# Batch 0's softmax on [(h n), tokens] rows, with its sums and its spreads by matmul

## The chip, the cores and the metric

The kernel runs on one NeuronCore of a Trainium2 chip. The metric is the time of one execution on the device, in microseconds (us). The core has five engines that work side by side, each through its own instructions in order: PE (TensorE, matrix products into PSUM), DVE (VectorE), ACT (ScalarE), POOL (GpSimd) and SP (SyncE, which only issues transfers here). PEld in the profile is the loading of PE's weights, which overlaps PE.

## The reference

Per batch b and head h there are 512 tokens of 64 values (`x`) and 32 state rows of 64 values (`state`). Attention runs both ways between them, and what both read goes through a two-layer network with a leaky ReLU.

```python
B, H, S, Ns, D = (8, 8, 512, 32, 64)
scores = scale * np.matmul(x, state.transpose(0, 1, 3, 2))
scores = scores - scores.max(-1, keepdims=True)
a = np.exp(scores)
a /= a.sum(-1, keepdims=True) + 1e-09
xread = np.matmul(a, state)
scores2 = scale * np.matmul(state, x.transpose(0, 1, 3, 2))
...
sread = np.matmul(a2, x)
attn = np.concatenate([xread, sread], axis=2)
...
h = x @ w_in          # x: attn as rows of H*D = 512; w_in is 512 x 2048
g = np.maximum(0.01 * h, h)
return g @ w_out      # w_out is 2048 x 512
```

The change is in the first of the two softmaxes: for each token and head, over the 32 state rows, for batch 0 alone.

## The kernel before, in words

All of it is one hand-written order: the order in the text is the order on each engine, and a tile framework adds the semaphores and the rotation of buffers. PSUM has four names with buffers (`tag`): `sc` (one buffer of two banks), `big` (one of two banks), `ph` and `py` (two of one bank each). A new tile of a tag waits until the old one in its buffer has been read.

The first layer never forms `xread`. Per batch and group of four heads g, the 128 rows (head, state row), written (h n), hold the probabilities `aT` [128 rows, 512 tokens], and `M` = state times `w_in` [128 rows, 2048] is made by `a_m(a, c, tag)` in four blocks c of 512 columns (eight 64*32 matmuls each) and copied to SBUF in bf16 by `m_evict(a, c, pm, copy)`, where `copy` names the engine (`VEC`, `SCA`). The first layer is then, per 128 columns of w_in, two matmuls of `M` and `aT` that add in PSUM, and a leaky ReLU on ACT. The second layer is cut into `piece`s: tile i of 128 tokens, quarter jq of the 16 blocks, four matmuls each.

From batch 1 on, scores stand in PSUM as [(h n), tokens] (`a_scores`), and VectorE finds the maximum and the sum over 32 rows with 32x32 transposes (`a_shift`, `a_probs`: L216, L224, L226, L238, L242, L245, L247, L248; `a_max2`, L266 and L268, is of the second softmax).

Batch 0's start is on its own lines. Its x comes in two halves (`x0_half`, `xt0_evict`). `scores0(u)` puts the scores of head group u with tokens on partitions (`sct`, [128 tokens, 16 pairs of token tile and head, 32 state rows]). VectorE then takes the maximum over the last axis (`max0`, L454) and subtracts it (`sub0`, L459), ACT takes the exponential (`exp0`, L463), VectorE sums (L467), adds 1e-9 (L468), takes the reciprocal (L471) and multiplies (L473, all in `probs0`). The result has tokens on partitions, so PE transposes it (`at0_t`, L477) and a copy on ACT or DVE brings it to `a0.aT` (L520, L546). `spin(n, tag)` issues n matmuls of zeros (L126) in places where PE would stand still. Between these stand the transposes of all states (`state_t`, L155, and `state_evict`, L164), which the scores and M of batches 1 to 7 need, and blocks of M of batches 0 and 1.

The first layer of batch 0 starts with g=0 for the first pair of columns as soon as half of `aT` is there, and with g=1 when the other half is (`ff1_0`, L533). Then come pairs j = 2, 4, ... 14, whose PSUM is `big` for j = 2, 6, 10 (one ACT instruction for both, L554) and two `ph` banks otherwise (two, L540). Between the pairs stand blocks of M (batch 0: c = 2 after j=2, c = 3 after j=6; batch 1: c = 2 after j=10, c = 3 after j=12; all copied by VectorE) and batch 0's second scores. After the loop come the casts of batch 1's x (`cast_x`, L99, half on DVE, half on POOL), its transposes (L188, copies L579), its scores, its softmax on DVE, and 56 matmuls of `piece` around them; then batch 1's first layer (`ff1`, L347) starts. Batch 2's x is cast on POOL (L99) when it has come.

Loads of the weights and of x for batches 1 and 2 are issued by POOL (L112, L118, L93), in this order: four of w_in with two casts between, one of w_out, x of batch 1, three of w_out, x of batch 2.

Of the kernel before, what the change touches and what calls it, by code (L numbers as in the profile page):

```python
# [9 lines left out]
P = 128  # L10
B, H, S, D = 8, 8, 512, 64
NS = 32
# [3 lines left out]
NT = S // P  # L16
NK = H // 2
SCALE = 1.0 / (D ** 0.5)

BF16 = mybir.dt.bfloat16  # L20
FP32 = mybir.dt.float32
AF = mybir.ActivationFunctionType
ALU = mybir.AluOpType
AX = mybir.AxisListType
# [3 lines left out]
def kernel(  # L28
# [9 lines left out]
    nc = tc.nc  # L38

    consts = ctx.enter_context(tc.tile_pool(name="consts", bufs=1))  # L40
    wpool = ctx.enter_context(tc.tile_pool(name="wpool", bufs=1))
    xpool = ctx.enter_context(tc.tile_pool(name="xpool", bufs=4))
    att = ctx.enter_context(tc.tile_pool(name="att", bufs=2))
# [3 lines left out]
    psum = ctx.enter_context(tc.tile_pool(name="psum", bufs=2, space=bass.MemoryType.PSUM))  # L47
# [5 lines left out]
    VEC, SCA, POO = nc.vector.tensor_copy, nc.scalar.copy, nc.gpsimd.tensor_copy  # L53
# [22 lines left out]
    ident = consts.tile([P, P], BF16, name="ident")  # L76
# [3 lines left out]
    for u in range(2):  # L80
        for g in range(2):
# [2 lines left out]
                ident[:].rearrange("p (k v q) -> p k v q", k=NK, v=2)[:, 2 * u:2 * u + 2, g],  # L84
            )

    w_in_bf = wpool.tile([P, NK, DFF], BF16, name="w_in_bf")
    w_out_bf = wpool.tile([P, 16, DM], BF16, name="w_out_bf")
    xs, xl = {}, {}

    def load_x(b, eng):
        xl[b] = xpool.tile([P, H, NT * D], FP32, name="xl", tag="xl", bufs=2)
        eng.dma_start(xl[b][:], x[b].rearrange("h (p t) d -> p h (t d)", t=NT))  # L93

    def open_xb(b):
        xs[b] = xpool.tile([P, NT, H, D], BF16, name="xb", tag="xb")
# [24 lines left out]
        )  # L121

    def spin(n, tag):
        p = psum.tile([P, S], FP32, name="pspin", tag=tag)
        for _ in range(n):
            nc.tensor.matmul(p[:], lhsT=idle[:, :P], rhs=idle[:], start=True, stop=True)  # L126

# [2 lines left out]
    stbd = consts.tile([P, NK, 2, NS], BF16, name="stbd")  # L130
# [43 lines left out]
    def a_open(a, b):  # L174
        a.b = b
        a.xb = xs[b]
        a.xT = att.tile([P, NT, NK, P], BF16, name="xT", tag="xT")
# [79 lines left out]
    def a_exp(a):  # L257
        a.e1 = block_exp(a.sh, NB)

    def a_probs(a):  # L260
        a.aT = att.tile([P, 2, S], BF16, name="aT", tag="aT")
        block_probs(a.aT[:], a.e1, NB)
# [51 lines left out]
    def a_m(a, c, tag):  # L314
        if c == 0:
            a.M = mpool.tile([P, 2, DFF], BF16, name="M", tag="M")
        if tag == "py":
            pm = [psum.tile([P, DM], FP32, name="pm", tag="py") for _ in range(2)]
            at = [t[:] for t in pm]
        else:  # L320
            pm = psum.tile([P, 2, DM], FP32, name="pm", tag=tag, bufs=1)
            at = [pm[:, g, :] for g in range(2)]
        for k in range(NK):
            for g in range(2):
                v, r = (k // 2, 2 * (k % 2) + (g ^ (k // 2))) if a.b == 0 else (g, k)
                nc.tensor.matmul(  # L326
                    at[v][NS * r:NS * (r + 1)],
                    lhsT=st_of(a, g, k),
                    rhs=w_in_bf[D * g:D * (g + 1), k, DM * c:DM * (c + 1)],
                    start=True, stop=True,  # L330
                )
        return pm

    def m_evict(a, c, pm, copy):
        cols = slice(DM * c, DM * (c + 1))
        if isinstance(pm, list):
            for g in range(2):
                copy(a.M[:, g, cols], pm[g][:])
        else:
            copy(a.M[:, :, cols], pm[:])  # L340
# [65 lines left out]

    att_of = [Attn() for _ in range(B)]
    a0, a1, a2 = att_of[:3]  # L410
    NG = NT * NK
# [24 lines left out]
    def scores0(u):  # L436
        for v in range(2):
            for t in range(NT):
                c = NK * t + 2 * v
                nc.tensor.matmul(  # L440
                    sct[u][:, c:c + 2, :].rearrange("p c n -> p (c n)"),
                    lhsT=a0.xT[:, t, 2 * u + v, :],
                    rhs=stbd[:, 2 * u + v].rearrange("p g n -> p (g n)"),
                    start=True, stop=True,
                )

    sh0, e10, at0 = {}, {}, {}

    def spread(v):
        return v[:, :, None].to_broadcast([P, NG, NS])  # L450

    def max0(u):
        m = att.tile([P, NG], FP32, name="m0", tag="m0")
        nc.vector.tensor_reduce(out=m[:], in_=sct[u][:], axis=AX.X, op=ALU.max)  # L454
        return m

    def sub0(u, m):
        sh0[u] = att.tile([P, NG, NS], FP32, name="sh0", tag="sh0")
        nc.vector.tensor_tensor(out=sh0[u][:], in0=sct[u][:], in1=spread(m), op=ALU.subtract)  # L459

    def exp0(u):
        e10[u] = att.tile([P, NG, NS], BF16, name="e0", tag="e0")
        nc.scalar.activation(out=e10[u][:], in_=sh0[u][:], func=AF.Exp, scale=SCALE)  # L463

    def probs0(u):
        r = att.tile([P, NG], FP32, name="r0", tag="r0")
        nc.vector.tensor_reduce(out=r[:], in_=e10[u][:], axis=AX.X, op=ALU.add)  # L467
        nc.vector.tensor_scalar(out=r[:], in0=r[:], scalar1=1e-9, scalar2=None, op0=ALU.add)  # L468
        q = att.tile([P, NG], BF16, name="q0", tag="q0")
        with nc.allow_low_precision(reason="one rounding, of the finished reciprocal"):  # L470
            nc.vector.reciprocal(q[:], r[:])  # L471
        at0[u] = att.tile([P, NG, NS], BF16, name="at0", tag="at0")
        nc.vector.tensor_tensor(out=at0[u][:], in0=e10[u][:], in1=spread(q), op=ALU.mult)  # L473

    def at0_t(u, t0, t1, dst):
        for t in range(t0, t1):
            nc.tensor.transpose(  # L477
                dst[:, P * (t - t0):P * (t - t0 + 1)],
                at0[u][:, NK * t:NK * (t + 1)].rearrange("p c n -> p (c n)"), ident[:],
            )  # L480

    load_w_in(0)
    load_w_in(1)
# [11 lines left out]
    for c in range(1, 4):  # L495
        load_w_out(c)
    load_x(2, nc.gpsimd)
    scores0(0)
    pxt = x0_half(1)
    m = max0(0)  # L500
    xt0_evict(1, pxt, (SCA, VEC))
    sub0(0, m)
    spin(2, "ph")
    scores0(1)
    exp0(0)
    spin(2, "ph")
    state_evict(state_t(), SCA)
    sub0(1, max0(1))
    exp0(1)
    m_evict(a0, 0, a_m(a0, 0, "py"), SCA)  # L510
    spin(3, "ph")
    open_xb(1)
    a_open(a1, 1)
    pm1 = a_m(a1, 0, "sc")
    spin(4, "ph")
    probs0(0)
    a0.aT = att.tile([P, 2, S], BF16, name="aT", tag="aT")
    pat = [psum.tile([P, 2, 2 * S], BF16, name="pat", tag="big", bufs=1)]
    at0_t(0, 0, NT, pat[0][:, 0])
    SCA(a0.aT[:, 0], pat[0][:, 0, :S])  # L520
    m_evict(a1, 0, pm1, SCA)
    probs0(1)
    pm = a_m(a0, 1, "py")

    h0 = hpool.tile([P, 16, S], BF16, name="hT", tag="hT")

    def ff1_0(banks, j, gs=(0, 1)):  # L530
        for g in gs:
            for v in range(2):
                nc.tensor.matmul(  # L533
                    banks[v], lhsT=a0.M[:, g, P * (j + v):P * (j + v + 1)], rhs=a0.aT[:, g, :],
                    start=(g == 0), stop=(g == 1),
                )

    def act_0(banks, j):
        for v in range(2):
            nc.scalar.activation(out=h0[:, j + v, :], in_=banks[v], func=AF.Prelu, alpha=0.01)  # L540

    ph = [psum.tile([P, S], FP32, name="ph", tag="ph")[:] for _ in range(2)]
    ff1_0(ph, 0, (0,))
    m_evict(a1, 1, a_m(a1, 1, "sc"), SCA)
    at0_t(1, 0, NT, pat[0][:, 1])
    VEC(a0.aT[:, 1], pat[0][:, 1, :S])  # L546
    m_evict(a0, 1, pm, VEC)
    ff1_0(ph, 0, (1,))
    act_0(ph, 0)
    for j in range(2, 16, 2):  # L550
        if j % 4 == 2 and j < 12:
            pr = psum.tile([P, 2, S], FP32, name="php", tag="big", bufs=1)
            ff1_0([pr[:, 0], pr[:, 1]], j)
            nc.scalar.activation(out=h0[:, j:j + 2, :], in_=pr[:], func=AF.Prelu, alpha=0.01)  # L554
        else:
            ph = [psum.tile([P, S], FP32, name="ph", tag="ph")[:] for _ in range(2)]
            ff1_0(ph, j)
            act_0(ph, j)
        if j in (2, 6):
            c = 2 + j // 4  # L560
            m_evict(a0, c, a_m(a0, c, "py"), VEC)
        elif j == 4:
            a_scores(a0)
            a_max2(a0)
        elif j in (10, 12):
            c = 2 + (j - 10) // 2
            m_evict(a1, c, a_m(a1, c, ("py", "big")[c - 2]), VEC)

    tags = ("py", "py", "ph", "ph")
    for g in range(2):  # L570
# [12 lines left out]
    a_max2(a1)  # L583
    piece(0, h0, 3, 0, tags[3])
    a_exp(a1)
    for g in range(2):
        a_exp2(a1, g)
    a_probs(a1)
    for jq in (1, 2):
        for i in range(NT):  # L590
            piece(0, h0, i, jq, tags[i])
    for i in (2, 3):
        piece(0, h0, i, 3, tags[i], VEC if i % 2 else SCA)
    a_probs2(a0)
# [144 lines left out]
```

## Time and profile before

| | us |
|---|---|
| median of 3 runs | 220.92 (220.80 to 221.04) |
| the profiled execution | 220.83 |
| its span, first to last instruction | 219.0 |
| PE busy in the span | 211.8 |
| DVE, ACT, POOL busy | 104.0, 136.2, 23.7 |
| granted PE clock over the span | 1.000 |
| batch 0's first layer, second half of its first pair, starts | 15.74 |
| x of batch 1 has come, POOL's cast starts | 24.21 |
| x of batch 2 has come, POOL's cast starts | 34.51 |
| batch 1's first layer starts | 38.89 |

Times in the profile are from the start of the span. A row of the timeline gives start and duration of one or several like instructions of an engine, its line, what it writes and reads, the shape (partitions x elements, for PE also the tile of the array, 128*128 when it is all of it) and, in brackets, how long the engine had stood idle and what ended that.

### The profile page before, as it was taken

The page shows a single profiled execution, that of the slowest core. Times are in us where ns is not written, and L with a number is a line of the kernel's source. Part 1 is how long each engine was busy: PE and PEld are TensorE (multiplying, and loading weights), DVE is VectorE, ACT ScalarE, POOL GpSimd, SP SyncE. Part 2 cuts the span into 40 slices and gives each one's busy share as a digit, 9 for nine tenths or more (in the row PEclk, how much of TensorE's full clock was granted, in tenths as well). Part 3 has the DMA queues.
Part 4 walks back from the last instruction along what each step waited for, and adds up shares of the span by engine and source line. Part 5 has one row for each costly group of instructions (what it writes and reads, how often), then busy time and mean ns, then how long its engine had stood idle before and what let it go on. Part 6 is the DMA issues. An engine that isn't in the chain of part 4 may idle for free.

```text
span 219.0 us, 3570 instructions
## 1 busy us (share of the span) xinstructions
PE 211.8 (97%) x1457; PEld 97.9 (45%) x1457; DVE 104.0 (47%) x150; ACT 136.2 (62%) x255; POOL 23.7 (11%) x31
## 2 busy tenths in 40 slices
PE   7879999999999999999999999999999999999993
PEld 2533444444454444434444444444444445466553
DVE  1877689799567318732865266624673000000000
ACT  4578805579968656964786477747684665554420
POOL 6850103003020011000200030000000000000000
PEclk9999999999999999999999999999999999999999
DMA  6999990696921892169216971271113111111113
GB/s 204 251 206 281 218 283 11 173 243 149 272 82 48 167 219 96 48 136 248 97 48 75 244 163 49 59 136 48 48 59 89 48 48 51 48 47 52 48 48 96
DMA packets 35311, 27.02 MB, mean 123 GB/s; under 512 B 19808, under 2 KB 30432, under 8 KB 35296
## 3 DMA queue, kind: packets, MB, share of 16 engines
q1 hardware_dynamic: 30384, 20.45, 35.1%
q0 software_dynamic: 4768, 6.29, 14.2%
q8 instruction: 11, 0.18, 0.3%
q10 hardware_dynamic: 144, 0.07, 0.2%
q14 instruction: 4, 0.03, 0.0%
HBM read 17.37 MB, written 8.91 MB: 120 GB/s over the span
## 4 chain that ended last, share of the span: by engine, by line
PE 84%; DVE 5%; DMA 5%; ACT 3%; issue 1%; SPq 1%; POOL 0%; ACTq 0%; DVEq 0%
PE py L375 47%; PE ph L347 22%; PE pm L326 4%; PE ph L358 3%; DMA w_in_bf<-in_moe_w_in_dram 3%; PE ph L533 2%; PE psr L300 1%; PE sc L206 1%; DMA st0f<-in_state_dram 1%; PE php L533 1%; ACT hT L352 1%; PE pspin L126 1%; DMA out_dram<-ysb 1%; PE pxt L188 1%; DVE xT L579 1%; DVE mrow L216 1%
## 5 line engine op out<-in xcount | busy, mean ns | idle before, releaser
L375 PE MATMUL py<-w_out_bf,hT 128*128 128x512 bf16 x496 | 125.7, 380 | 0.0
L352 ACT ACTIVATE hT<-ph 128x512 bf16<-128x512 f32 x112 | 67.0, 601 | 44.8 <-PE ph L347 44.8
L375 PEld LDWEIGHTS <-hT 128*128 128x128 bf16 x496 | 46.6, 98 | 57.2 <-issue 5.8
L347 PE MATMUL ph<-aT,M 128*128 128x512 bf16 x224 | 66.1, 379 | 0.6 <-ACT hT L352 0.3
L347 PEld LDWEIGHTS <-M 128*128 128x128 bf16 x224 | 21.5, 98 | 27.6 <-issue 1.9
L381 ACT COPY ysb<-py 128x512 f32<-128x512 f32 x31 | 18.1, 585 | 12.7 <-PE py L375 12.7
L340 DVE CAST M<-pm 128x1024 bf16<-128x1024 f32 x12 | 14.7, 1223 | 21.9 <-PE pm L326 21.9
L99 POOL CAST xb<-xl 128x2048 bf16<-128x2048 f32 (+1 forms) x7 | 12.4, 1772 | 103.3 <-DMA xl<-in_x_dram 48.5
L403 DVE COPY ysh<-pyh 128x256 f32<-128x256 f32 x1 | 0.4, 424 | 44.8 <-PE pyh L398 44.8
L216 DVE TRANSPOSE_TENSOR_REDUCE mrow<-sc 128x32 f32<-128x1024 f32 x7 | 8.7, 1250 | 20.7 <-PE sc L206 20.6
L340 ACT CAST M<-pm 128x1024 bf16<-128x1024 f32 x15 | 15.2, 1013 | 1.1 <-PE pm L326 1.0
L238 DVE TRANSPOSE_TENSOR_REDUCE r<-e 128x32 f32<-128x1024 bf16 x7 | 8.7, 1244 | 9.8 <-ACT e L233 9.8
L274 ACT ACTIVATE e<-sc,mcols 128x512 bf16<-128x512 f32 x16 | 11.1, 698 | 0.4 <-DVE mcols L268 0.3
L233 ACT ACTIVATE e<-sh 128x1024 bf16<-128x1024 f32 x7 | 7.3, 1049 | 5.6 <-DVE sh L226 5.6
L326 PE MATMUL pm<-w_in_bf,st_t 64*32 64x512 bf16 x224 | 10.2, 382 | 0.3 <-ACT M L340 0.3
L266 DVE TENSOR_REDUCE mcol<-sc 128x2 f32<-128x1024 f32 x8 | 9.7, 1214 | 0.1
L362 ACT ACTIVATE hs<-ph 128x256 bf16<-128x256 f32 x16 | 6.0, 384 | 4.6 <-PE ph L358 4.4
L247 DVE STREAM_TRANSPOSE qb<-qh 128x1024 bf16<-128x1024 bf16 x7 | 8.7, 1245 | 0.2
L224 DVE STREAM_TRANSPOSE mrowb<-mrow 128x1024 f32<-128x1024 f32 x7 | 8.7, 1245 | 0.2
L126 PE MATMUL pspin<-idle 128*128 128x512 bf16 x21 | 7.6, 496 | 1.2 <-DVE warm L74 1.2
L226 DVE TENSOR_TENSOR sh<-sc,mrowb 128x1024 f32<-128x1024 f32 x7 | 8.6, 1224 | 0.2
L358 PE MATMUL ph<-sr_t,w_in_bf 128*128 128x256 bf16 x64 | 8.3, 273 | 0.0
(81 smaller groups left out, 140.8 us busy)
## 6 DMA issues: line engine op xcount, KB each, us to landing
out_dram<-ysb SPq DMA_DIRECT2D x31, 256.0 KB, 2.3
xl<-in_x_dram SPq DMA_DIRECT2D x5, 1024.0 KB, 6.7
w_in_bf<-in_moe_w_in_dram POOLq DMA_DIRECT2D x4, 512.0 KB, 8.7
w_out_bf<-in_moe_w_out_dram POOLq DMA_DIRECT2D x4, 512.0 KB, 16.5
xl<-in_x_dram POOLq DMA_DIRECT2D x2, 1024.0 KB, 17.7
xf<-in_x_dram SPq DMA_DIRECT2D x2, 512.0 KB, 4.6
stf<-in_state_dram SPq DMA_DIRECT2D x1, 512.0 KB, 5.8
out_dram<-ysb SPq DMA_DIRECT2D x8, 64.0 KB, 1.7
```

The lines of the kernel that those rows point to most:

```text
L99: copy(xs[b][:, :, h0:h1].rearrange("p t h d -> p h t d"), xl[b][:, h0:h1].rearrange("p h (t d) -> p h t d", t=NT),)
L126: nc.tensor.matmul(p[:], lhsT=idle[:, :P], rhs=idle[:], start=True, stop=True)
L216: nc.vector.tensor_reduce(out=m1[:], in_=flat.rearrange("p (c j) -> p c j", j=NS), axis=AX.X, op=ALU.max, apply_transpose=True,)
L266: nc.vector.tensor_reduce(out=m2[:], in_=a.sc[:], axis=AX.X, op=ALU.max, negate=True)
L274: nc.scalar.activation(out=a.e2[:, g], in_=a.sc[:, g, :], func=AF.Exp, bias=a.m2s[:, g:g + 1], scale=SCALE, accum_out=a.r2[:, g:g + 1],)
L326: nc.tensor.matmul(at[v][NS * r:NS * (r + 1)], lhsT=st_of(a, g, k), rhs=w_in_bf[D * g:D * (g + 1), k, DM * c:DM * (c + 1)], start=True, st ...
L340: copy(a.M[:, :, cols], pm[:])
L347: nc.tensor.matmul(ph[:], lhsT=a.M[:, g, P * j:P * (j + 1)], rhs=a.aT[:, g, :], start=(g == 0), stop=(g == 1),)
L352: nc.scalar.activation(out=hT[:, j, :], in_=ph[:], func=AF.Prelu, alpha=0.01)
L358: nc.tensor.matmul(ph[:, :n], lhsT=w_in_bf[:, k, P * j:P * (j + 1)], rhs=sr_t[:, k, :], start=(k == 0), stop=(k == NK - 1),)
L375: nc.tensor.matmul(y.py[:], lhsT=hT[:, j, P * i:P * (i + 1)], rhs=w_out_bf[:, j, :], start=(j == 0), stop=(j == 15),)
L381: copy(ysb[:], y.py[:])
```

## The change

It takes batch 0's softmax off the layout with tokens on partitions, but for the search of the maximum. In words:

- `rows0(u)` makes the same scores a second time, as [(h n), tokens] rows in PSUM (`scn`, four 128*32 matmuls of 512 columns).
- `max0` takes the negated maximum from `sct` as before. `split0` writes it as the sum of two bf16 values. `spread0` adds both to `scn` by matmuls: for each token tile and head, one column of 128 tokens, repeated 32 times as weights, times the identity: 32 matmuls of 128*32 weights and 128 columns per head group.
- `exp0` reads `scn` from PSUM on ACT, and its result is already in the layout of `aT`.
- `sum0` sums over the 32 rows by four matmuls with `ones4` (a block of ones per head, new constant, five memsets on POOL) and puts tokens on partitions; `recip0` adds 1e-9 and takes the reciprocal on VectorE; `recip0_rows` spreads it with 16 matmuls of `spread0`; `probs0` multiplies on VectorE straight into `a0.aT`. The eight transposes and two copies go.
- Spins in this stretch: 1, 1 and 2 in place of 2, 2, 3 and 4.
- The first layer of batch 0 starts with whole pairs; `big` is used for j = 0, 4, 8.
- Blocks of M: block 1 of both batches was made ahead of the first layer and now comes inside it. Batch 0: c = 1 after j=0, 2 after j=4, 3 after j=8. Batch 1: c = 0 before the loop as now, its copy on VectorE after j=0 (it was on ACT); c = 1 after j=10 (in `py`), 2 after j=12 (in `big`), 3 among the pieces (copied by ACT).
- `a_probs(a1)` now stands ahead of `a_exp2(a1)`; these are on different engines.

The core of the diff:

```diff
-    def sub0(u, m):
-        sh0[u] = att.tile([P, NG, NS], FP32, name="sh0", tag="sh0")
-        nc.vector.tensor_tensor(out=sh0[u][:], in0=sct[u][:], in1=spread(m), op=ALU.subtract)
+    def rows0(u):
+        scn[u] = psum.tile([P, S], FP32, name="scn", tag="ph")
+        for c in range(NK):
+            nc.tensor.matmul(
+                scn[u][NS * c:NS * (c + 1), :], lhsT=stbd[:, 2 * u + c // 2, c % 2, :],
+                rhs=a0.xT[:, :, 2 * u + c // 2, :], start=True, stop=False,
+            )
+
+    def spread0(dst, parts, start):
+        for t in range(NT):
+            for i, part in enumerate(parts):
+                for c in range(NK):
+                    nc.tensor.matmul(
+                        dst[NS * c:NS * (c + 1), P * t:P * (t + 1)],
+                        lhsT=part[:, NK * t + c:NK * t + c + 1].to_broadcast([P, NS]),
+                        rhs=ident[:], start=start, stop=start or (t == NT - 1 and i == 1),
+                    )
...
+    def split0(m):
+        hi = att.tile([P, NG], BF16, name="hi0", tag="hi0")
+        VEC(hi[:], m[:])
+        lo = att.tile([P, NG], BF16, name="lo0", tag="lo0")
+        with nc.allow_low_precision(reason="the second of two parts of one fp32 value"):
+            nc.vector.tensor_tensor(out=lo[:], in0=m[:], in1=hi[:], op=ALU.subtract)
+        return hi, lo
...
+    def sum0(u):
+        r0[u] = psum.tile([P, NG], FP32, name="r0", tag="ph")
+        for t in range(NT):
+            nc.tensor.matmul(
+                r0[u][:, NK * t:NK * (t + 1)], lhsT=e10[u][:, P * t:P * (t + 1)], rhs=ones4[:],
+                start=True, stop=True,
+            )
...
+    def recip0_rows(u, q):
+        qb0[u] = psum.tile([P, S], FP32, name="qb0", tag="ph")
+        spread0(qb0[u], (q,), True)
+
+    def probs0(u):
+        nc.vector.tensor_tensor(out=a0.aT[:, u], in0=e10[u][:], in1=qb0[u][:], op=ALU.mult)
...
     scores0(0)
     pxt = x0_half(1)
     m = max0(0)
     xt0_evict(1, pxt, (SCA, VEC))
-    sub0(0, m)
-    spin(2, "ph")
+    rows0(0)
     scores0(1)
+    m = split0(m), max0(1)
+    rows0(1)
+    spread0(scn[0], m[0], False)
     exp0(0)
-    spin(2, "ph")
+    spin(1, "py")
+    spread0(scn[1], split0(m[1]), False)
+    exp0(1)
+    sum0(0)
+    q = recip0(0)
     state_evict(state_t(), SCA)
-    sub0(1, max0(1))
-    exp0(1)
+    recip0_rows(0, q)
+    sum0(1)
+    q = recip0(1)
     m_evict(a0, 0, a_m(a0, 0, "py"), SCA)
...
+    probs0(0)
+    spin(1, "big")
+    recip0_rows(1, q)
+    probs0(1)
     pm1 = a_m(a1, 0, "sc")
...
+    spin(2, "big")
...
-    for j in range(2, 16, 2):
-        if j % 4 == 2 and j < 12:
+    for j in range(0, 16, 2):
+        if j % 4 == 0 and j < 12:
...
+        if j == 0:
+            m_evict(a0, 1, a_m(a0, 1, "py"), VEC)
+            m_evict(a1, 0, pm1, VEC)
+        elif j in (4, 8):
+            m_evict(a0, 1 + j // 4, a_m(a0, 1 + j // 4, "py"), VEC)
+        elif j == 6:
             a_scores(a0)
             a_max2(a0)
         elif j in (10, 12):
-            c = 2 + (j - 10) // 2
-            m_evict(a1, c, a_m(a1, c, ("py", "big")[c - 2]), VEC)
+            c = 1 + (j - 10) // 2
+            m_evict(a1, c, a_m(a1, c, ("py", "big")[c - 1]), VEC)
...
     a_exp(a1)
+    a_probs(a1)
+    for i in range(NT):
+        piece(0, h0, i, 1, tags[i])
+    m_evict(a1, 3, a_m(a1, 3, "big"), SCA)
     for g in range(2):
         a_exp2(a1, g)
-    a_probs(a1)
-    for jq in (1, 2):
-        for i in range(NT):
-            piece(0, h0, i, jq, tags[i])
+    for i in range(NT):
+        piece(0, h0, i, 2, tags[i])
```

More of the change, by code (lines that the diff above doesn't have):

```diff
@@ L85 @@
             )
+    ones4 = consts.tile([P, NK], BF16, name="ones4")
+    nc.gpsimd.memset(ones4[:], 0.0)
+    for c in range(NK):
+        nc.gpsimd.memset(ones4[NS * c:NS * (c + 1), c:c + 1], 1.0)
     w_in_bf = wpool.tile([P, NK, DFF], BF16, name="w_in_bf")
@@ L123, in spin @@
     def spin(n, tag):
-        p = psum.tile([P, S], FP32, name="pspin", tag=tag)
+        p = psum.tile([P, S], FP32, name="pspin", tag=tag, bufs=2 if tag in ("ph", "py") else 1)
         for _ in range(n):
@@ L445, in scores0 @@
                 )
-    sh0, e10, at0 = {}, {}, {}
-    def spread(v):
-        return v[:, :, None].to_broadcast([P, NG, NS])
+    scn, e10, r0, qb0 = {}, {}, {}, {}
+    def rows0(u):
[8 more added lines that the diff above has]
+            for i, part in enumerate(parts):
+                for c in range(NK):
+                    nc.tensor.matmul(
[3 more added lines that the diff above has]
+                    )
@@ L452, in max0 @@
     def max0(u):
         m = att.tile([P, NG], FP32, name="m0", tag="m0")
-        nc.vector.tensor_reduce(out=m[:], in_=sct[u][:], axis=AX.X, op=ALU.max)
+        nc.vector.tensor_reduce(out=m[:], in_=sct[u][:], axis=AX.X, op=ALU.max, negate=True)
         return m
-    def sub0(u, m):
-        sh0[u] = att.tile([P, NG, NS], FP32, name="sh0", tag="sh0")
-        nc.vector.tensor_tensor(out=sh0[u][:], in0=sct[u][:], in1=spread(m), op=ALU.subtract)
-    def exp0(u):
-        e10[u] = att.tile([P, NG, NS], BF16, name="e0", tag="e0")
-        nc.scalar.activation(out=e10[u][:], in_=sh0[u][:], func=AF.Exp, scale=SCALE)
@@ L465, in probs0 @@
[L465 to L468, printed above, removed]
+    def split0(m):
[5 more added lines that the diff above has]
+        return hi, lo
@@ new lines, in exp0, with recip0 @@
+    def exp0(u):
+        e10[u] = att.tile([P, S], BF16, name="e0", tag="e0")
+        nc.scalar.activation(out=e10[u][:], in_=scn[u][:], func=AF.Exp, scale=SCALE)
+    def sum0(u):
[5 more added lines that the diff above has]
+            )
+    def recip0(u):
+        r = att.tile([P, NG], FP32, name="rs0", tag="rs0")
+        nc.vector.tensor_scalar(out=r[:], in0=r0[u][:], scalar1=1e-9, scalar2=None, op0=ALU.add)
@@ L471, in probs0 @@
             nc.vector.reciprocal(q[:], r[:])
[L472 to L480, printed above, removed]
+        return q
+    def recip0_rows(u, q):
[3 more added lines that the diff above has]
+        nc.vector.tensor_tensor(out=a0.aT[:, u], in0=e10[u][:], in1=qb0[u][:], op=ALU.mult)
     load_w_in(0)
@@ L497 @@
     load_x(2, nc.gpsimd)
+    a0.aT = att.tile([P, 2, S], BF16, name="aT", tag="aT")
+    open_xb(1)
+    a_open(a1, 1)
     scores0(0)
@@ L501, with ff1_0 @@
     xt0_evict(1, pxt, (SCA, VEC))
-    sub0(0, m)
-    spin(2, "ph")
+    rows0(0)
     scores0(1)
+    m = split0(m), max0(1)
+    rows0(1)
+    spread0(scn[0], m[0], False)
     exp0(0)
-    spin(2, "ph")
+    spin(1, "py")
[3 more added lines that the diff above has]
+    q = recip0(0)
     state_evict(state_t(), SCA)
-    sub0(1, max0(1))
-    exp0(1)
+    recip0_rows(0, q)
+    sum0(1)
+    q = recip0(1)
     m_evict(a0, 0, a_m(a0, 0, "py"), SCA)
-    spin(3, "ph")
-    open_xb(1)
-    a_open(a1, 1)
+    probs0(0)
+    spin(1, "big")
+    recip0_rows(1, q)
+    probs0(1)
     pm1 = a_m(a1, 0, "sc")
[L515 to L523, printed above, removed]
+    spin(2, "big")
     h0 = hpool.tile([P, 16, S], BF16, name="hT", tag="hT")
-    def ff1_0(banks, j, gs=(0, 1)):
-        for g in gs:
+    def ff1_0(banks, j):
+        for g in range(2):
             for v in range(2):
@@ L536, in ff1_0 @@
                 )
[L538 to L549, printed above, removed]
-    for j in range(2, 16, 2):
-        if j % 4 == 2 and j < 12:
+    for j in range(0, 16, 2):
+        if j % 4 == 0 and j < 12:
             pr = psum.tile([P, 2, S], FP32, name="php", tag="big", bufs=1)
@@ L555 @@
         else:
[L556 to L562, printed above, removed]
+            ph = [psum.tile([P, S], FP32, name="ph", tag="ph") for _ in range(2)]
+            ff1_0([p[:] for p in ph], j)
+            for v in range(2):
+                nc.scalar.activation(out=h0[:, j + v, :], in_=ph[v][:], func=AF.Prelu, alpha=0.01)
+        if j == 0:
[4 more added lines that the diff above has]
+        elif j == 6:
             a_scores(a0)
```

## The prediction

> **What bounds the kernel now.** I read the page first, then the busy time by stage, then the timeline of the first 40 us, and last the rows of single tiles.
>
> ```profile
> span 219.0 us, 3570 instructions
> ...
> PE 211.8 (97%) x1457; PEld 97.9 (45%) x1457; DVE 104.0 (47%) x150; ACT 136.2 (62%) x255; POOL 23.7 (11%) x31
> ```
>
> TensorE is the bound: 7.2 us of the span are not PE. Which part the change can reach shows in the table by stage (stretch, its length, then busy time and instruction count for PE, PEld, DVE, ACT, POOL, then clock, DMA share, GB/s):
>
> ```profile
> 5.00:10.00 5.00, 4.54 (x71) 2.60 (x69) 4.11 (x8) 2.46 (x6) 4.04 (x6) 1.00 1.16 268
> 10.00:16.00 6.00, 4.62 (x51) 1.97 (x52) 4.81 (x11) 5.00 (x7) 4.16 (x6) 1.00 1.24 206
> 16.00:25.00 9.00, 8.76 (x71) 3.10 (x70) 7.33 (x12) 7.52 (x12) 0.79 (x1) 1.00 1.18 259
> 25.00:39.00 14.00, 13.66 (x82) 6.32 (x80) 11.74 (x14) 5.39 (x12) 2.14 (x2) 1.00 0.65 150
> ...
> 80.00:200.00 120.00, 120.00 (x776) 54.37 (x775) 48.16 (x64) 79.08 (x149) 5.68 (x3) 1.00 0.34 90
> ```
>
> The change lies between 7.5 and 39 us. From 80 to 200 us PE never pauses and its instructions there are the same in both kernels, so the result is the shift of one moment: when batch 1's first-layer loop (L347) starts, 38.89 us. The timeline (start, duration, engine, line, operation, tiles, wait in brackets) shows what leads there:
>
> ```profile
> 4.29 0.42 PE L140 MATMUL pst<-identg,stb 128*64 128x128 bf16 x4
> 9.25 0.69 PE L155 MATMUL pst<-ident,stb 128*64 128x64 bf16 x32
> 10.47 0.82 PE L126 MATMUL pspin<-idle 128*128 128x512 bf16 x3
> 12.87 0.39 DVE L468 TENSOR_SCALAR r<-r 128x16 f32<-128x16 f32 x1
> 15.74 0.59 PE L533 MATMUL ph<-aT,M 128*128 128x512 bf16 x2 [0.59 <-DVE aT L546]
> 24.21 1.04 POOL L99 CAST xb<-xl 128x1024 bf16<-128x1024 f32 x1 [10.05 <-DMA xl<-in_x_dram]
> 24.89 1.89 PE L375 MATMUL py<-w_out_bf,hT 128*128 128x512 bf16 x8
> 29.09 1.25 DVE L216 TRANSPOSE_TENSOR_REDUCE mrow<-sc 128x32 f32<-128x1024 f32 x1 [0.54 <-PE sc L206]
> 34.05 0.17 DVE L268 TENSOR_SCALAR mcols<-mcol 128x2 f32<-128x2 f32 x1
> 34.51 1.89 POOL L99 CAST xb<-xl 128x2048 bf16<-128x2048 f32 x1 [9.26 <-DMA xl<-in_x_dram]
> 35.39 1.04 DVE L242 TENSOR_SCALAR r<-r 128x32 f32<-128x32 f32 x1
> 38.89 1.19 PE L347 MATMUL ph<-aT,M 128*128 128x512 bf16 x4 [0.27 <-DVE aT L248]
> ```
>
> Two things meet at 38.89. PE's pieces end at 38.62. Batch 1's softmax on VectorE ends at 38.84. Inside that softmax L242 takes 1.04 us where the median of its seven instances is 0.18, and ends with POOL's cast (36.40): while the cast runs, this VectorE operation doesn't. POOL's cast starts when x of batch 2 lands, 34.51, a transfer whose queue the change leaves as it is. So the softmax has slack on the early side: it can start up to 0.9 us earlier (34.51 - 35.39) and still end at 38.84.
>
> **The change, part by part.** First the unknown: one tiled 128*32 matmul. Batch 0's maximum and reciprocal are spread by 32+32+16+16 = 96 matmuls of 128 columns on four column tiles. Nearest rows: in L155, two column tiles, 32 matmuls start over 0.69-0.196 (one's duration) = 0.49 us, 16 ns each. In L188 sixteen full-width 128-column matmuls go in 0.89 us of the chain, 56 ns each; four tiles at once make 14. L140's four matmuls (two tiles, 128 columns) start over 0.42-0.31 = 0.11 us while the spins beside them go 0.43 apart for 512 columns, twice the later 0.2155: two tiles do run at once. Bounds: 14 ns (four at once) and 56 (none at once); 29 if only two go at once. I take 16, the row of column tiles that is nearest.
>
> [...]
>
> Switching shape: four full matmuls then eight tiled take 0.96 us start to start (17.47 to 18.43), 0.10 over 4 x 0.2155; the eight 64*32 ones take 0.34 to the next start, 0.13 over one pass. So a tiled group of eight costs 0.44 in all.
>
> *Start of batch 0's first layer.* Before, its second half starts at 15.74. After, by steps. The row scores (four matmuls of 512 columns, 0.22 if parallel as L326, 0.86 if not) take the place of a spin in the wait for xT, and follow the second scores, ending near 9.0. VectorE: the bf16 half of the first maximum is ready to go at 8.50, waits for POOL's cast of the states (7.66 to 8.71) as L242 does, 8.73 to 8.90; rest 9.10; second maximum 9.07 to 9.76 (9.02 before); its halves at 0.17 each 9.96 and 10.16 (L468's 0.39 beside POOL's DMA issues says up to 0.2 more). PE: first spread 9.0 to 9.6, spin, second spread 10.06, waiting for the last half, to 10.67; exp 10.93 to 11.52. Then PE is in a row without slack: four small sums 0.23, state transposes 0.61, spread of the reciprocal 0.36, sums 0.23, M 0.44, spin 0.22, second spread 12.85 to 13.11, M 0.31, two spins 0.56, and 0.2 until the last spin, whose bank the first layer takes, is finished: 14.25. Both softmax products on VectorE (0.69 each, 13.35 and 14.03) and M's copies on ScalarE (13.9) are ready by then. A ns per small matmul is worth 0.1 us here.
>
> *Work from there.* Before, from 15.74: 30 first-layer matmuls, 56 of the pieces (0.2155 each), 16 transposes 0.89, six tiled groups 2.64: 37.81, and 1.08 of waits to 38.89. After: 32, 56, the transposes, eight groups 3.52 (M's blocks 1 of both batches came before): 14.25 + 6.90 + 12.07 + 0.89 + 3.52 = 37.63. So 1.49 us earlier a start is 0.18 earlier an end, if nothing else waits. But copies of M now stand on VectorE inside the loop that did not: those of batch 0's block 1 (two, 0.60 from one start to the next) come only after j=0, and batch 1's block 0 (1.22) moves there from ScalarE. j=4 waits 0.18 for the second half of block 1. Block 1 of batch 1 now takes the `py` banks right behind block 3 of batch 0, whose copies stand behind the 1.22 maximum: copies at about 20.7 and 21.3, free at 22.0, where PE is ready at 21.4: 0.58. Sum 0.76. Bounds: 0, and 1.2 if ScalarE falls behind too.
>
> *Where it shows.* First piece before: 15.74 + 6.47 + 5 x 0.44 = 24.41 and 0.48 of waits = 24.89. After: 14.25 + 6.90 + 6 x 0.44 + 0.48 + 0.76 = 25.03, 0.14 later. Batch 1's scores and maximum are 0.14 later (29.23), mcols at 34.19, still ahead of the cast at 34.51; L242 waits for the cast's end as now, and aT is ready at 38.84 as now. PE's pieces end at 38.62 + 0.14 + 0.44 (M's block 3 of batch 1 now stands among them) = 39.20. The start of L347 moves from 38.89 to 39.20: +0.31. What VectorE is rid of (two subtractions of 0.69 and two sums of 0.68, 2.72 us), the eight transposes with their two copies (0.59, 0.42) and seven of eleven spins are in the walk to 14.25 already and buy nothing more at the end, since the loop behind it is held by copies of M, and batch 1 by its x (24.21). The five new memsets on POOL (0.1 each) lie in its 1.27 us wait for st0f. No DMA is added or moved.
>
> **Sum.** The profiled execution took 220.83 us (span 219.0 and 1.8 around it); +0.31 is 221.14. The median of the runs is 220.92, 0.09 higher, so the forecast is **221.25 us**. 0.2% is 0.44 us, about what a measurement can tell from no change: the forecast is inside, near its edge.
>
> **Rivals.**
>
> *The cast gets in front of mcols (slower).* For: its margin is 34.51 - 34.19 = 0.32 us, and 0.2 of waiting for DMA issues or 3 ns more per small matmul eat it. Against: the sum above. If mcols comes after 34.51 it waits for 36.43; then, with the rows' own steps, L238 36.50 to 37.75, L242 0.20, L245 0.38, L247 1.28, L248 0.70: aT at 40.3, L347 at 40.35, +1.45: **222.4**. It decides at 0.32 us more delay. [...]
>
> *Small matmuls two at a time, 29 ns (slower).* 96 x 13 ns = 1.25 us later at 14.25, so mcols late too, 40.35 from VectorE, and PE's own end 39.20 + 1.25 = 40.45, plus copies that then meet the DVE chain: +1.6 to 3, **223**. For: 128*32 has no row. Against: L326, four columns at once. At 56 ns, 3.8 us: 225 or more.
>
> *The change pays (faster).* Without the new waits (0.76) and with the spins cut short, the first piece could come 0.9 earlier and L242 ahead of the cast; PE's 37.63 and 0.48 of waits would then set the start: 38.1, -0.8: **220.1**. Against: batch 1's x lands at 24.21 whatever happens; cast to 25.25, two halves of transposes and copies bring scores to about 27.75, 0.86 earlier than now: L242 would still meet the cast. Short of that, the start stays at 38.89.
>
> *The gain is hidden and nothing is added.* aT is ready at 38.84 either way; without the copies' waits PE is ready too: **220.9**. This is the lower part of the forecast's own range.
>
> **How the numbers follow.** Forecast's case 0.50, with its own range 220.8 to 221.6; of it 0.16 is above +0.44. Cast in front 0.26. Slow matmuls 0.14. Faster 0.10. Slower 0.16+0.26+0.14 = 0.56, same 0.34, faster 0.10. The range leaves out the faster rival and most of the slow matmuls: 220.7 to 222.6.
>
> **What would show it.** Right: spreads of 32 matmuls in 0.5 to 0.7 us; first `php` near 14.25; PE waiting for DVE's copies near 22; mcols before POOL's second cast, L242's counterpart long again; L347's counterpart at 39.2, and no difference grown behind it. Wrong: spreads over 0.9 us; mcols 2 us late with ACT's exp behind it; or the first piece before 24.5.

## The result and the profile after

| | before | after |
|---|---|---|
| median of 22 runs each | 220.91 (220.72 to 222.21) | 221.69 (221.41 to 222.86) |
| ratio, 95% interval | | 1.0034 (1.0023 to 1.0045) |
| the profiled execution | 220.83 | 221.45 |
| its span | 219.0 | 219.7 |

The change makes the kernel slower by a third of a per cent: 0.78 us between the medians, 0.62 between the profiled executions. The forecast, 221.25 (+0.33), had the side and one of the causes; it is 0.44 us short. Here and below, ratios leave out runs that are more than 1.5% above the fastest of their kernel.

First the page of the kernel after, span and busy time of each engine:

```profile
span 219.7 us, 3742 instructions
...
PE 210.6 (96%) x1529; PEld 98.5 (45%) x1554; DVE 103.5 (47%) x150; ACT 134.7 (61%) x253; POOL 24.4 (11%) x36
```

It then gives the table by stage, with columns as in the prediction:

```profile
5.00:10.00 5.00, 4.03 (x74) 2.33 (x73) 4.10 (x9) 1.84 (x4) 4.36 (x7) 1.00 1.17 266
10.00:16.00 6.00, 5.67 (x137) 3.03 (x138) 2.75 (x9) 3.88 (x6) 4.45 (x6) 1.00 1.24 207
16.00:25.00 9.00, 8.56 (x67) 2.87 (x67) 8.36 (x13) 6.72 (x12) 0.76 (x1) 1.00 1.17 256
25.00:39.00 14.00, 13.82 (x87) 6.26 (x87) 11.74 (x13) 6.23 (x13) 2.18 (x2) 1.00 0.67 153
80.00:200.00 120.00, 118.69 (x761) 54.36 (x775) 48.19 (x64) 78.89 (x150) 5.68 (x3) 1.00 0.35 92
```

VectorE is rid of 2.06 us between 10 and 16 us (4.81 to 2.75) and gets 1.03 between 16 and 25 (7.33 to 8.36), where the copies of M now stand. From 80 to 200 us PE has 761 matmuls on record against 776, but the weight loads are 775 in both: 15 matmul records are missing from the trace, and the lower busy time (118.69) is no pause. PE's busy time on the page is lower for the same reason in part.

The timeline of after, the rows that answer to those of before, with some that decided:

```profile
4.15 1.63 POOL L117 DMA_DIRECT2D w_in_bf<-in_moe_w_in_dram  x2 [0.24 <-issue]
...
8.12 0.93 DVE L480 CAST hi<-m 128x16 bf16<-128x16 f32 x1
...
9.44 0.23 PE L467 MATMUL scn<-ident,lo 128*32 128x128 bf16 x4
9.49 0.23 PE L467 MATMUL scn<-ident,hi 128*32 128x128 bf16 x4
...
11.02 0.70 PE L160 MATMUL pst<-ident,stb 128*64 128x64 bf16 x32
...
14.18 1.02 PE L567 MATMUL php<-aT,M 128*128 128x512 bf16 x4
...
21.43 0.94 PE L331 MATMUL pm<-w_in_bf,st_t 64*32 64x512 bf16 x8
...
24.93 1.89 PE L380 MATMUL py<-w_out_bf,hT 128*128 128x512 bf16 x7
...
29.14 1.25 DVE L221 TRANSPOSE_TENSOR_REDUCE mrow<-sc 128x32 f32<-128x1024 f32 x1 [0.54 <-PE sc L211]
...
33.42 0.41 PE L331 MATMUL pm<-w_in_bf,st_t 64*32 64x512 bf16 x8
...
34.09 0.17 DVE L273 TENSOR_SCALAR mcols<-mcol 128x2 f32<-128x2 f32 x1
...
35.16 1.89 POOL L104 CAST xb<-xl 128x2048 bf16<-128x2048 f32 x1 [9.87 <-DMA xl<-in_x_dram]
35.44 1.65 DVE L247 TENSOR_SCALAR r<-r 128x32 f32<-128x32 f32 x1
...
39.40 0.68 DVE L386 COPY ysb<-py 128x512 f32<-128x512 f32 x1
39.54 1.19 PE L352 MATMUL ph<-aT,M 128*128 128x512 bf16 x4 [0.42 <-DVE aT L253]
...
40.57 1.02 PE L380 MATMUL py<-w_out_bf,hT 128*128 128x512 bf16 x4
```

Batch 0's first layer starts at 14.18, where before the second half of its first pair started at 15.74. At the first piece nothing of that is left: 24.93 against 24.89. By an estimate with the lengths that the prediction took from before's rows, 0.87 of it goes to work that now stands behind the start (two matmuls and one block of M), and the rest to PE's waits: 0.53 for the copies near 22 (the block at 21.43 takes 0.94 instead of 0.41), and some 0.2 inside the second pair, which starts at 15.47. Up to mcols (34.09 against 34.05) the two kernels are level. Then comes the loss: a block of M between the pieces (33.42), a longer VectorE operation under the cast (L247, 1.65 against L242's 1.04), and L352 at 39.54 against 38.89.

The last row is the first piece inside batch 1's first layer. Two rows of before belong beside it:

```profile
38.75 0.69 DVE L381 COPY ysb<-py 128x512 f32<-128x512 f32 x1
...
39.91 1.02 PE L375 MATMUL py<-w_out_bf,hT 128*128 128x512 bf16 x4
```

The piece is 0.66 later (40.57 - 39.91). From there to the end of the span it is 179.1 us in both, and within 0.1 us the same in the profile of every run below: all of the difference between the profiles arises before 40.6 us.

### The profile page after: what moved, and what is told of

The parts are those of the page before. It is cut to its first block, busy times and chain, and to the rows that moved or that the text cites. A ratio compares the mean times of both kernels' runs of the same rounds, so it can differ in the third digit from the quotient of the medians.

```text
span 219.7 us, 3742 instructions
## 1 busy us (share of the span) xinstructions
PE 210.6 (96%) x1529; PEld 98.5 (45%) x1554; DVE 103.5 (47%) x150; ACT 134.7 (61%) x253; POOL 24.4 (11%) x36
## 4 chain that ended last, share of the span: by engine, by line
PE 83%; DVE 8%; ACT 3%; DMA 3%; issue 2%; SPq 1%; ACTq 0%
PE py L380 47%; PE ph L352 21%; PE pm L331 4%; PE ph L363 3%; DMA xf<-in_x_dram 2%; PE ph L567 2%; PE psr L305 1%; PE sc L211 1%; DVE mcol L271 1%; ACT hT L357 1%; PE php L567 1%; DVE r L247 1%; DMA out_dram<-ysb 1%; PE scn L467 1%; PE pxt L193 1%
## 5 line engine op out<-in xcount | busy, mean ns | idle before, releaser
L380 PE MATMUL py<-w_out_bf,hT 128*128 128x512 bf16 x480 | 122.9, 380 | 1.7 <-issue 1.1
L352 PE MATMUL ph<-aT,M 128*128 128x512 bf16 x217 | 64.7, 379 | 1.0 <-DVE aT L253 0.4
L352 PEld LDWEIGHTS <-M 128*128 128x128 bf16 x224 | 21.5, 98 | 27.8 <-issue 1.9
L345 DVE CAST M<-pm 128x1024 bf16<-128x1024 f32 x13 | 15.9, 1224 | 21.9 <-PE pm L331 21.9
L345 ACT CAST M<-pm 128x1024 bf16<-128x1024 f32 x14 | 14.2, 1012 | 0.5 <-PE pm L331 0.5
L363 PEld LDWEIGHTS <-w_in_bf 128*128 128x128 bf16 x64 | 6.3, 98 | 2.4
```

The source lines that it names most:

```text
L352: nc.tensor.matmul(ph[:], lhsT=a.M[:, g, P * j:P * (j + 1)], rhs=a.aT[:, g, :], start=(g == 0), stop=(g == 1),)
L363: nc.tensor.matmul(ph[:, :n], lhsT=w_in_bf[:, k, P * j:P * (j + 1)], rhs=sr_t[:, k, :], start=(k == 0), stop=(k == NK - 1),)
L380: nc.tensor.matmul(y.py[:], lhsT=hT[:, j, P * i:P * (i + 1)], rhs=w_out_bf[:, j, :], start=(j == 0), stop=(j == 15),)
```

## The experiments

All are read by one measure beside the time: from the start of batch 1's scores on PE (what the prologue and the first loop lead to) to that piece. The stretch between is free of what happened earlier, but for the landing of x of batch 2, whose cast falls into it.

| run | median (lowest to highest) | ratio to before, 95% | scores, piece | between |
|---|---|---|---|---|
| before | 220.91 | | 28.61, 39.91 | 11.30 |
| after | 221.69 | 1.0034 (1.0023, 1.0045) | 28.65, 40.57 | 11.92 |
| e1 after, ones4 by VectorE | 221.97 (221.48 to 222.21) | 1.0036 (1.0023, 1.0049) | 28.91, 40.58 | 11.67 |
| e2 before, with the memsets | 222.65 (220.98 to 225.95) | 1.0043 (1.0023, 1.0064) | 28.66, 40.14 | 11.48 |
| e3 after, no 1e-9 | 221.73 (221.45 to 222.71) | 1.0032 (1.0021, 1.0043) | 28.92, 40.59 | 11.67 |
| e4 before, no 1e-9 | 220.94 (220.72 to 221.21) | 0.9995 (0.9986, 1.0003) | 28.94, 40.16 | 11.22 |
| e5 after, cast late | 221.70 (221.21 to 221.96) | 1.0030 (1.0019, 1.0041) | 28.65, 40.32 | 11.67 |
| e6 before, cast late | 220.84 (220.66 to 221.37) | 0.9996 (0.9988, 1.0005) | 29.28, 40.50 | 11.22 |
| e7 e6 and pieces reordered | 220.63 (220.48 to 221.08) | 0.9983 (0.9975, 0.9992) | 28.66, 39.71 | 11.05 |
| e8 e5 and pieces reordered | 221.15 (220.43 to 221.85) | 1.0004 (0.9993, 1.0014) | 28.94, 40.09 | 11.15 |
| e9 before, cast after aT, reordered | 220.48 (220.18 to 221.99) | 0.9974 (0.9956, 0.9993) | 28.95, 39.66 | 10.71 |
| e10 after, likewise | 220.95 (220.93 to 221.68) | 0.9992 (0.9974, 1.0010) | 29.46, 40.62 | 11.16 |
| e11 e10 without the block | 220.75 (220.24 to 221.62) | 0.9978 (0.9961, 0.9995) | 29.33, 40.04 | 10.71 |
| e12 e10, block earlier | 220.58 (220.30 to 221.10) | 0.9975 (0.9960, 0.9989) | 29.00, 39.70 | 10.70 |

Ratios go against runs of before beside them (median 221.02 to 221.04; highest 222.74). One run of e3, 440.65 us, stands apart from all others and is left aside here.

**The memsets (e1, e2).** The first load of w_in is issued at 4.15 us in after, 3.77 in before, and x of batch 2 is cast later. e1 takes the five memsets of `ones4` off POOL, e2 puts them alone into the kernel before.

```diff
-    nc.gpsimd.memset(ones4[:], 0.0)
+    nc.vector.memset(ones4[:], 0.0)
...
-        nc.gpsimd.memset(ones4[NS * c:NS * (c + 1), c:c + 1], 1.0)
+        nc.vector.memset(ones4[NS * c:NS * (c + 1), c:c + 1], 1.0)
```

> The changed kernel with its five small memsets (ones4) on VectorE instead of POOL. Theory (the memsets made POOL's first weight load go out 0.38 us late, batch 2's x came 0.65 late, and the cast of it held the softmax of batch 1 until 37.05 instead of 36.40): first w_in issue back at about 3.8, POOL's cast of batch 2's x at 34.5, the held tensor_scalar ends at 36.4, batch 1's first layer starts when PE is done with its pieces, about 39.15; +0.25 us over before, not +0.75. Rival (VectorE's small casts, or the matmuls, are what costs): cast still at 35.1, start at 39.5, +0.7.

> The kernel before with the same five memsets on POOL and nothing else; their tile is not used. Theory: first w_in issue about 0.4 late, batch 2's x 0.65 late, batch 1's first layer at 39.5; +0.65 us. Rival (memsets are hidden in POOL's wait for the state, as the prediction said): no change, 38.89.

e1 moved the issue (3.90) and x of batch 2 (cast at 34.37), cut L247 to 0.61 and the stretch to 11.67, and still took 221.97 (median of only five runs): this speaks against the memsets as what the median of after pays. e2 speaks for them: its ratio, 1.0043, is as large as that of the whole change. But its runs spread over 5 us, which the one profile, of a run of 221.0, can't explain; its cast came at 34.73. Every kernel with the memsets on POOL issued at 4.15 to 4.46 with an idle of 0.24 or 0.25 put down to "issue", every other at 3.77 to 4.10. The landing of x of batch 2 differs by 0.36 between two kernels without these memsets on POOL (34.51 and 34.87 in before and e4), by 0.22 between before and e2, and by 0.65 between before and after, so what the memsets do to it stays open, as do e2's long runs.

**The operation under the cast (e3, e4).** The add of 1e-9 (L247 in after, L242 in before) is left out in batch 1's first softmax, in both kernels.

```diff
-        nc.vector.tensor_scalar(out=r1[:], in0=r1[:], scalar1=1e-9, scalar2=None, op0=ALU.add)
+        if eps:
+            nc.vector.tensor_scalar(out=r1[:], in0=r1[:], scalar1=1e-9, scalar2=None, op0=ALU.add)
...
-        block_probs(a.aT[:], a.e1, NB)
+        block_probs(a.aT[:], a.e1, NB, a.b != 1)
```

> The changed kernel without the addition of 1e-9 in batch 1's first softmax (the held instruction); batch 1 alone leaves it out, and sums there are at least about 1, so it is below fp32's resolution. Theory (the hold of that one instruction carries the loss): reciprocal follows the sum at once at 35.45, aT at about 37.8, start set by PE's own end at about 39.15; +0.25 over before. Rival (PE's own work or a later stage carries it): +0.7 as the changed kernel. Third way: the reciprocal is held by the cast as well, then +0.6.

> The kernel before without that addition in batch 1 alone. Theory: aT at about 37.75, PE's pieces end at 38.62 and set the start: -0.25 us. If the reciprocal is held too: 0 to +0.05.

Neither time moved, though aT was ready long before PE came. The timeline of e4 shows what takes over:

```profile
37.39 0.69 DVE L249 TENSOR_TENSOR aT<-e,qb 128x1024 bf16<-128x1024 bf16 x1
38.79 0.59 PE L348 MATMUL ph<-aT,M 128*128 128x512 bf16 x2
38.99 0.69 DVE L382 COPY ysb<-py 128x512 f32<-128x512 f32 x1 [0.91 <-PE py L376]
...
39.73 0.59 PE L348 MATMUL ph<-aT,M 128*128 128x512 bf16 x2 [0.35 <-DVE ysb L382]
```

aT is ready at 38.08, and PE starts the layer at 38.79 without waiting. But its second pair of matmuls waits 0.35 for VectorE's copy of the last piece, which frees the PSUM bank. In before the same copy stood at 38.75, right behind aT, and the second pair began when it ended. So the wait for aT had hidden another, 0.08 us shorter (11.30 - 11.22). From scores to piece the stretch without a wait for aT is 11.22 with before's pieces (e4, e6) and 11.67 with after's (e1, e3, e5): the 0.45 of the block of M between the pieces, in full.

**The cast itself (e5 on after, e6 on before).** POOL's cast of batch 2's x is put behind the reciprocal of batch 1's softmax: a copy of one column of it on POOL stands ahead of the cast.

```diff
+    gate = att.tile([P, 1], BF16, name="gate", tag="gate", bufs=1)
+    POO(gate[:], last_q[0][:, :1])
     cast_x(2, 0, 8, POO)
```

> The changed kernel; POOL's cast of batch 2's x first waits for the reciprocal of batch 1's softmax (a copy of one column of it), so that it can hold no VectorE operation of that softmax. Theory P (PE's end carries the loss: the block of M among the pieces is 0.44 us, and the copy of the last piece on VectorE, which frees the bank for the second step of batch 1's first layer, follows PE's end): that step's piece starts at 40.3 to 40.6, about 11.67 after batch 1's scores; fastest runs 221.2 to 221.4, the long runs of 222 to 222.9 disappear; +0.45 to +0.5 over the kernel of the next label. Theory H (the hold carries it): as fast as before, 220.9.

> The kernel before with the same late cast. Theory P: 11.22 from batch 1's scores to that piece, no change of the median against before (220.9), since PE's end plus the copy sets it already. Theory H: 0.1 to 0.3 faster than before.

e6 is level with before, e5 with after. The add takes 0.18 again in both; the stretch is 11.22 and 11.67 as with e4 and e3. The hold under the cast thus costs what stood beyond those: 0.08 in the profile of before, 0.25 in that of after, and nothing in after's median.

**The hidden wait taken away (e7, e8).** On top of the late cast, the last two pieces that are copied are put ahead of two others, so that the copies end before PE does (on e6, e7, shown here; the same on e5, e8).

```diff
-    for jq in (1, 2):
-        for i in range(NT):
-            piece(0, h0, i, jq, tags[i])
-    for i in (2, 3):
-        piece(0, h0, i, 3, tags[i], VEC if i % 2 else SCA)
+    for i in range(NT):
+        piece(0, h0, i, 1, tags[i])
+    for jq in (2, 3):
+        for i in (2, 3):
+            piece(0, h0, i, jq, tags[i], VEC if i % 2 else SCA)
+    for i in (0, 1):
+        piece(0, h0, i, 2, tags[i])
```

> As e6, and the two pieces whose copies free the ph banks (tiles 2 and 3, last quarter) come ahead of two third-quarter pieces of tiles 0 and 1, 8 matmuls or 1.7 us earlier. If the wait for the copy on VectorE is what follows PE's end (theory P), the first steps of batch 1's layer run on without it: -0.3 to -0.45 us against e6, 220.5; if batch 1's aT is the end instead (at 38.8), nothing or little.

> The same two edits on the changed kernel. Theory P: 220.9 to 221.0, still 0.45 behind e7 by the block of M among the pieces. Theory H: as fast as e7.

e8 gained 0.55 on e5 (0.52 in the stretch); e7 gained 0.21 on e6 (0.17), less than expected. In e7 the wait is for aT again, because the cast, moved back, meets another operation of VectorE:

```profile
36.20 1.90 POOL L99 CAST xb<-xl 128x2048 bf16<-128x2048 f32 x1
37.32 1.31 DVE L251 TENSOR_TENSOR aT<-e,qb 128x1024 bf16<-128x1024 bf16 x1
38.56 0.68 DVE L384 COPY ysb<-py 128x512 f32<-128x512 f32 x1
38.69 1.19 PE L350 MATMUL ph<-aT,M 128*128 128x512 bf16 x4
```

The product takes 1.31 instead of 0.69: it ends at 38.63, 0.53 behind the end of the cast (38.10).

**Both holds away (e9, e10).** The cast waits for aT instead, and ACT makes both copies (on before, e9; the same edits on after, e10).

```diff
-            piece(0, h0, i, jq, tags[i], VEC if i % 2 else SCA)
+            piece(0, h0, i, jq, tags[i], SCA)
...
-    POO(gate[:], last_q[0][:, :1])
+    POO(gate[:], a1.aT[:, 0, :1])
```

> The kernel before with both things removed that stood between PE's end and batch 1's first layer: POOL's cast of batch 2's x waits for the finished aT of batch 1, so it holds nothing of that softmax; and the last quarters of tiles 2 and 3 come ahead of the third quarters of tiles 0 and 1, both copied by ACT, so that no step waits for their copies. Expected: from batch 1's scores to the first piece in its layer 10.87 us (44 matmuls, then four, no wait) in place of 11.22 to 11.30; 220.5, -0.35 to -0.45 against before.

> The changed kernel with the same edits. Theory P: 0.44 more from scores to that piece than e9, 11.31, for the block of M among the pieces and nothing else; 220.95, 0.45 behind e9. If the hold had carried the loss of the change: 10.87, equal to e9.

The timeline of e9:

```profile
37.62 0.69 DVE L248 TENSOR_TENSOR aT<-e,qb 128x1024 bf16<-128x1024 bf16 x1
...
38.50 1.90 POOL L99 CAST xb<-xl 128x2048 bf16<-128x2048 f32 x1
38.62 2.18 DVE L285 TENSOR_SCALAR a<-e,qc 128x512 bf16<-128x512 bf16 x2
38.80 1.03 PE L347 MATMUL ph<-aT,M 128*128 128x512 bf16 x4
39.66 1.03 PE L375 MATMUL py<-w_out_bf,hT 128*128 128x512 bf16 x4
```

PE runs from the pieces through both pairs into the next piece without a wait. The cast now holds the products of the second softmax (2.18 for two; 0.62 in before), which nobody awaits then. With nothing else left in the stretch, the two kernels differ by 0.45 in it (11.16 and 10.71), the length of the block of M, and by 0.47 in the median.

**The block itself (e11, e12, both on e10).** e11 leaves its matmuls out, and ACT copies block 2 in its place, so that batch 1's output is not the reference's. e12 (shown here) makes the block ahead of batch 1's scores, where PE stands waiting for the copy of batch 1's transposed x.

```diff
     piece(0, h0, 2, 0, tags[2])
+    pm3 = a_m(a1, 3, "big")
     a_scores(a1)
...
-    m_evict(a1, 3, a_m(a1, 3, "big"), SCA)
+    m_evict(a1, 3, pm3, SCA)
```

> As e10 without the eight matmuls of block 3 of batch 1's M; ACT copies block 2 in its place, so the output for batch 1 is not the reference's. Theory P: 10.87 from scores to piece, as e9, 0.44 less than e10; time 220.5. What stays between it and e9 is the changed softmax itself (start of batch 0's first layer and the waits in its loop): 0 to 0.1.

> As e10 with that block made ahead of batch 1's scores, where PE waits some 0.2 us for the copy of the second half of batch 1's transposed x. Scores 0.2 later, scores to piece 10.87: net 0.2 less than e10, 220.75.

Without it the stretch is 10.71, as in e9: the block is the 0.45. The median of e11 missed its 220.5: it fell only 0.20 below e10, to 220.75, and stays 0.27 above e9, whose stretch is the same. This 0.27 is taken up below, under "Open".

Moved, the block is out of the stretch, which is 10.70; it then stands just ahead of it:

```profile
28.77 0.41 PE L331 MATMUL pm<-w_in_bf,st_t 64*32 64x512 bf16 x8
```

From the start of the piece in front of the scores to the scores it is 1.18 us in e12 (27.82 to 29.00) and 1.10 in e10 (28.36 to 29.46). So the block costs 0.08 there instead of 0.45, because most of it falls into a wait that was there; 0.2 had been expected. The median falls by 0.37 from e10, to 220.58. e9 and e12 both end below before, with intervals clear of 1, by the edits that they share; they are 0.10 apart. By these two medians the new softmax, with the block in that wait, costs about nothing and gains nothing.

## Why the prediction came out as it did

**Right.** The small matmuls: 32 of a spread start over some 0.6 us, groups of four 0.055 apart (9.44, 9.49), 14 ns each. The rival at 29 is out. The first layer at 14.18 (14.25 foretold); the hi half held by POOL's cast of the states (0.93 instead of the 0.17 of the second one; it ends at 9.05, the cast at 9.01); PE's wait for the copies near 22 (0.53 above the usual 0.41, foretold 0.58); the first piece at 24.93 (25.03), in part by luck, as said below; mcols at 34.09 (34.19), ahead of the cast; PE's pieces done at 39.12 (39.20), of it 0.45 for the block of M (0.44). From the layer's start on, the difference did not grow (0.65 there, 0.66 at the piece).

**Luck.** The prediction's sum of new waits, 0.76, came out at some 0.7, but one of its two terms is not in the trace. Pair j=4 was to wait 0.18 for the second half of block 1; it starts (16.54) right behind pair j=2. A pause of about the same length stands inside pair j=2 instead, and had not been foreseen. Also, the terms give 220.92 + 0.31 = 221.23; the 221.25 on record is 0.02 above them.

**The step that failed**, though the forecast held, is "so the result is the shift of one moment: when batch 1's first-layer loop (L347) starts, 38.89 us", and with it the term "from 38.89 to 39.20: +0.31". It took the 0.27 us that PE waited for aT as slack which the block could use up. The moment that carries is 0.6 us further on, the second pair, and it awaits PE's last piece plus one copy of it; there the slack was 0.08 (e4). So PE's later end passes on nearly whole. In the two profiles the +0.66 of the piece is made of the scores +0.04, the block +0.45, the hold in after +0.25, and less the hold in before, 0.08.

**A second step that failed** is "L242 waits for the cast's end as now", with x of batch 2 "a transfer whose queue the change leaves as it is": in after's profile that x came 0.65 later, and L247 ended at 37.09 instead of 36.43. e3 and e5, where nothing of this is left, show that it lengthens that stretch of the profile by 0.25 us (11.92 against 11.67) and not the median (221.73 and 221.70 against 221.69).

**Open** is the rest of the median's 0.78. The block gives 0.45. The same change of kernel costs 0.79 and 0.86 in e4 to e3 and e6 to e5, where the stretches differ by 0.45, and 0.52 in e7 to e8, where they differ by 0.10, but 0.47 in e9 to e10. e9 and e11, with equal stretches, are 0.27 apart. So 0 to 0.4 us is left beside the stretch and isn't there in every pair. As every profile takes the same time behind the piece, it lies, as far as profiles can tell, ahead of batch 1's scores. Those start at 28.61 to 29.28 in kernels with before's start, and at 28.65 to 29.46 with after's: one profile for each can't tell a shift from this spread.

The profiles do show one thing there that only the kernels with after's start have: the pause of PE inside pair j=2. It is longest in e10:

```profile
15.84 0.39 PE L567 MATMUL ph<-aT,M 128*128 128x512 bf16 x1
16.69 0.82 PE L567 MATMUL ph<-aT,M 128*128 128x512 bf16 x3 [0.46 <-issue]
```

From the start of pair j=2 to that of j=4 it is 1.04 to 1.09 us in five of these kernels, 1.27 in e11, 1.48 in e8 and 1.50 in e10, where two neighbouring pairs of before take 0.88 (20.08 to 20.96). So the same code loses 0.2 to 0.6 us here, and the part above 0.2 passes on: from the layer's start to the piece in front of the scores it is 13.35 to 13.41 in the five and 13.74 to 13.81 in the three (in e11 also by an x of batch 1 that came late), but 11.77 or 11.78, from the second half of the first pair, in all six with before's start. The profile puts the pause down to "issue", that is, to no wait that it shows. What it is, and how often it is long in the runs that were not profiled, stays open.

**The rivals.** No profile shows the cast in front of mcols; the nearest is e1, 34.37 behind 34.35. That mcols, an operation of 128x2, would wait there until 36.43 was the prediction's estimate from L242, of 128x32, and no run shows it; the smallest operation of VectorE that a run shows held by a cast is the hi half, of 128x16. The long runs of after (up to 222.86) may be of that kind; e5, where the cast cannot come early, has none above 221.96, which agrees and proves nothing with 7 runs; e9, where it cannot come early either, has one of 221.99, 1.5 above its median. The faster rival failed where the prediction had put it: the 1.56 us won at the start were gone by the first piece. "The gain is hidden and nothing is added" was refuted by the block.

## What to carry to other kernels

A wait that ends an idle stretch is slack only up to the next wait behind it: before crediting it, follow the path without it to the next instruction of the bound engine (here a copy that frees a bank, 0.08 us behind). Work moved onto the bound engine cost its length where that engine had no real gap, and little in a gap that stayed (0.45 among the pieces, 0.08 ahead of the scores). A start that is 1.5 us sooner buys nothing when work that stood ahead of it now stands behind it and copies further on hold the bound engine. And a profile shows one run: here the medians differ by 0.78 and the profiled runs by 0.62.

## What the runs showed of the hardware

- In these rows, of an operation of VectorE and one of POOL beside it, the one that began first held the other: VectorE's operation of 128x32 took 1.65 us instead of 0.18 beside POOL's cast (after; it ends at 37.09, the cast at 37.05); a product with both inputs in SBUF 1.31 instead of 0.69, ending 0.53 behind the cast (e7). It goes both ways: in e5 VectorE's half of batch 1's cast began first (24.93, POOL's 24.97) and took 0.69, and POOL's took 1.56 instead of 1.04. Other rows show no hold: the reciprocal of 128x32 took 0.35 us under the cast in e4 as elsewhere.
- Times of several kernels fall into steps of about 0.25 us: e3 at 221.45 to 221.46, 221.70 to 221.73, 221.95 to 221.97 and 222.24; e12 at 220.30, 220.57, 220.83, 221.10. Those of e4 do not: they lie evenly from 220.72 to 221.21. In the profiles batch 1's scores show steps too: 28.61 to 28.66 in five, 28.91 to 28.95 in five others. What makes the steps was not tried. A difference of medians that is smaller than a step can be one of how often each step was taken.
